# One ordered weight queue and half-by-half opening passes in a recurrent-attention kernel that is bound by the PE

## The chip, the cores and the metric

The kernel runs on one core of one Trainium2 chip. The metric is device time in microseconds (us), the median over several executions. Executions of one and the same kernel differ by up to 8 us of 1260 here (0.6%), so differences of a few us are read in two ways: from ratios over interleaved rounds with a 95% interval, and from fixed landmarks in the trace of one execution. PE is the matmul engine, DVE the vector engine, ACT the scalar engine, SP the engine that issues most DMAs. The granted clock is the share of its full speed at which the PE was allowed to run.

## The reference

A layer norm, a recurrent attention with 8 memory tokens over 64 segments of 32 tokens, a residual, then a gated feed-forward with its own norm and residual. What matters is the recurrence: the memory of a segment is the attention output of the one before.

```python
for s in range(n_seg):                       # 64 segments, strictly in order
    xs = x[:, s * seg_len:(s + 1) * seg_len, :]
    h = concatenate([mem, xs], axis=1)       # 8 memory tokens + 32 tokens, 640 wide
    q, k, v = h @ Wq, h @ Wk, h @ Wv         # 32 heads of 128, bfloat16
    p = softmax(where(mask, q @ k.T * scale, -1e9))
    o = (p @ v) @ Wo
    mem = o[:, :M, :]                        # feeds the next segment
    outs.append(o[:, M:, :])
```

Wq, Wk, Wv and Wo are 5.24 MB each, 21 MB together. No segment can be finished before all four are on the chip.

## The kernel before

A small scheduler records every operation with the tiles that it reads and writes, and turns that into semaphore waits; so an operation waits for exactly the data it names. Each weight is loaded in two halves (heads 0 to 15 and 16 to 31). The opening loads:

```python
    for g in range(4):                                   # memory tokens, first on the sync queue
        dma(wtok[1][32 * g:32 * g + M, :, :], mem0_ap..., r=[("wtok", 1)], w=[("wtok0", g)])
    x0 = oTe[:]...
    ln1_load(-1, xt, ("xt",))                            # token rows 0..63
    ln1_load(0, x0, ("oTe", 0))                          # token rows 64..191
    srcs = (A_Wq, A_Wk, A_Wv)
    qs = ("sp", "act")
    for j in (1, 0, 2):                                  # K, Q, V
        for i in range(2):                               # halves: one on each queue
            dma(W[:, j, :, 2048 * i:2048 * i + 2048], srcs[j]..., w=[("W", j, i)], eng=qs[i])
    for i in range(2):
        dma(Wo[:, 16 * i:16 * i + 16, :], A_Wo..., w=[("Wo", i)], eng=qs[i])
```

The opening passes project three groups of tokens (the rows of segments 0 and 1, and pass 0: the 8 memory tokens with 24 rows of later segments, the riders, that fill up its 32 rows) with K, Q and V. One pass uses both halves of a weight at once, with one weight load for both; so nothing starts before both halves have landed:

```python
    for j in (1, 0):                                     # K, then Q
        for n, (a, ks) in enumerate(ex_act + [(a0, k0)]):
            project(a, ks, j, (0, 1), bks)               # both halves
            to_tok(bks[0], t, "act"); to_tok(bks[1], t + 1, "dve")
            trans8(tok[t], ..., bk)                      # waits for the two copies
            ...                                          # evacuate to K or Q storage
    for n, (a, ks) in enumerate(ex_act + [(a0, k0)]):
        project(a, ks, 2, (0, 1), bks)                   # V
        to_v(...); to_v(...)
    ...
    for s in range(NSEG):
        ...                                              # (s > 0: the projections of this segment)
        scores(s); exp_mem(); exp_x()
        pv_mem(s); trans_om(s)                           # memory values, normalized, transposed
        wo_pass(oT[par], ..., T1)                        # output projection: needs Wo half 0, then half 1
        to_act(s + 1, B(T1), ...)                        # DVE transpose: the memory of segment s + 1
```

The DVE transpose in `to_act` (into the tile TBf) is the landmark of this text: it ends the opening when it starts for segment 1, and there is one for each later segment.

The softmax here doesn't subtract the row's maximum and nothing guards it: scores larger than these inputs give would overflow.

## Time and profile before

| | before |
|---|---|
| median of 3 executions | 1268.34 us (1266.53 to 1270.35) |
| profiled span | 1262.6 us |
| first projection matmul | 30.88 us |
| first output projection | 64.50 to 68.46 us |
| transpose for segment 1, for segment 2 | 68.52, 83.32 us |
| transpose for segment 63 (954.1 us after that for segment 2) | 1037.44 us |

The page of the kernel before: busy time of each engine, then the busy tenths of the PE and of the DMA engines in 40 slices of 31.6 us each, then the chain that ended last.

```profile
PE 1176.5 (93%) x31431; PEld 661.4 (52%) x29111; DVE 611.0 (48%) x1497; ACT 408.4 (32%) x775; POOL 26.6 (2%) x94
...
PE   0889999999999999999999999999999997999998
...
DMA  9801000010110101010111010100000025110100
...
PE 86%; DMA 4%; DVE 4%; ACT 3%; issue 1%; SPq 1%; POOL 0%; DVEq 0%; ACTq 0%; POOLq 0%
```

The PE is the limit nearly everywhere. The exception is the first slice, where it does nothing and the DMA is at 9 tenths. The timeline of the opening (start in us, duration, engine or issuing queue, line, operation, tile; in brackets the idle time before it and what ended it):

```profile
0.83 0.42 ACTq L304 DMA_DIRECT2D W<-in_A_Wk_dram  x1
...
5.15 3.04 SPq L304 DMA_DIRECT2D wtok<-in_A_mem_dram  x4
...
9.45 0.43 SPq L304 DMA_DIRECT2D W<-in_A_Wk_dram  x1
...
30.88 0.62 PE L345 MATMUL ps<-W,act_r 128*32 128x512 bf16 x4 [8.53 <-DMA W<-in_A_Wk_dram]
...
64.50 3.96 PE L546 MATMUL ps<-Wo,oT 128*32 128x160 bf16 x128 [0.38 <-DVE oT L380]
...
68.52 0.35 DVE L466 STREAM_TRANSPOSE TBf<-ps 128x160 f32<-128x160 f32 x1 [4.08 <-PE ps L546]
```

The activation queue issues its half of K at 0.83 us and the sync queue its half only at 9.45 us, because its memory-token loads wait for a memset and are issued first. By then the other queue holds halves of Q, V and Wo too, and the second half of K shares the engines with them until 30.88 us.

The windows view of the same kernel (stretch, its length, busy us of PE, PEld, DVE, ACT, POOL with counts, granted clock, DMA share, GB/s):

```profile
6.00:8.00 2.00, 0.00 (x0) 0.00 (x0) 0.00 (x0) 0.00 (x0) 0.00 (x0) 1.00 1.01 401
16.00:28.00 12.00, 1.16 (x10) 0.74 (x10) 4.96 (x18) 0.99 (x4) 0.00 (x0) 1.00 1.03 410
48.00:56.00 8.00, 6.42 (x115) 2.17 (x64) 1.67 (x3) 3.03 (x4) 0.00 (x0) 1.00 1.07 363
57.00:58.50 1.50, 1.50 (x36) 0.39 (x16) 0.69 (x1) 0.30 (x1) 0.00 (x0) 1.00 0.15 55
58.50:60.00 1.50, 1.50 (x36) 0.36 (x16) 0.51 (x1) 0.60 (x1) 0.00 (x0) 1.00 0.00 0
64.50:67.50 3.00, 3.00 (x92) 3.00 (x96) 0.00 (x0) 0.00 (x0) 0.00 (x0) 0.50 0.41 106
```

The DMA is saturated, on one queue (6 to 8 us) as on two. Two lines will matter later: at 57 us the rate collapses but a tail at a share of 0.15 goes on to 58.5; and the first output projection ran at a granted clock of 0.50, after a stretch in which the PE had several short waits (the longest 1.11 us).

### The profile page before, as it was taken

What the parts mean: (1) busy time and instruction counts of PE and PEld (TensorE: products, weight loads), DVE (VectorE), ACT (ScalarE), POOL (GpSimd) and SP (SyncE); (2) the same over time, 40 slices, a digit from 0 to 9 for tenths busy, and PEclk for the clock granted to TensorE, in tenths of its full rate; (3) what the DMA queues carried; (4) which work ended last, traced back from release to release, by engine and by line L of the source; (5) the groups of instructions that cost most, each with busy time, mean ns of one, the idle gap of its engine ahead of it and who ended that gap; (6) DMA issues with size and microseconds to landing.
All of it is one profiled execution on the core that took longest, in us unless ns stands there. A gap on an engine that the chain in (4) does not pass through costs nothing.

```text
span 1262.6 us, 64636 instructions
## 1 busy us (share of the span) xinstructions
PE 1176.5 (93%) x31431; PEld 661.4 (52%) x29111; DVE 611.0 (48%) x1497; ACT 408.4 (32%) x775; POOL 26.6 (2%) x94
## 2 busy tenths in 40 slices
PE   0889999999999999999999999999999997999998
PEld 0255555555556555555555555555555554455454
DVE  2244545454545454555555555454545442543522
ACT  0323333333333333333333333333333321321311
POOL 1000000000000000000000000000000000000000
PEclk9999999999999999999999999999999998999999
DMA  9801000010110101010111010100000025110100
GB/s 364 310 21 24 21 23 21 23 23 22 23 24 21 25 19 25 21 44 19 43 22 44 21 44 20 24 20 23 20 21 20 19 99 183 37 63 22 43 21 21
DMA packets 47819, 60.03 MB, mean 48 GB/s; under 512 B 20224, under 2 KB 36288, under 8 KB 47552
## 3 DMA queue, kind: packets, MB, share of 16 engines
q1 hardware_dynamic: 43520, 45.41, 12.6%
q10 hardware_dynamic: 4032, 10.49, 2.2%
q8 instruction: 237, 3.88, 1.3%
q14 instruction: 30, 0.25, 0.1%
HBM read 36.79 MB, written 6.55 MB: 34 GB/s over the span
## 4 chain that ended last, share of the span: by engine, by line
PE 86%; DMA 4%; DVE 4%; ACT 3%; issue 1%; SPq 1%; POOL 0%; DVEq 0%; ACTq 0%; POOLq 0%
PE ps L345 32%; PE ps L546 12%; PE ps L331 9%; PE ps L884 9%; PE ps L364 6%; PE ps L912 5%; PE ps L488 3%; PE ps L372 2%; PE ps L558 2%; PE ps L521 2%; DVE TBf L466 2%; DMA W<-in_A_Wk_dram 2%; PE ps L583 2%; ACT Kr L378 1%; ACT Qr L378 1%
## 5 line engine op out<-in xcount | busy, mean ns | idle before, releaser
L345 PE MATMUL ps<-W,act_r 128*32 128x512 bf16 x6460 | 447.2, 381 | 39.0 <-DVE act_r L467 12.6
L345 PEld LDWEIGHTS ps<-W,act_r 128*32 128x32 bf16 x6460 | 162.9, 96 | 286.0 <-issue 84.4
L380 DVE CAST tok<-ps 128x512 bf16<-128x512 f32 x161 | 110.9, 689 | 154.8 <-PE ps L345 78.3
L378 ACT ACTIVATE tok<-ps 128x512 bf16<-128x512 f32 x161 | 95.9, 596 | 229.7 <-PE ps L331 187.8
L546 PE MATMUL ps<-Wo,oT 128*32 128x160 bf16 x8448 | 163.8, 236 | 3.1 <-issue 2.6
L546 PEld LDWEIGHTS ps<-Wo,oT 128*32 128x32 bf16 x8448 | 148.6, 98 | 12.7 <-issue 4.5
L331 PE MATMUL ps<-W,act_r 128*32 128x512 bf16 x1420 | 138.8, 381 | 0.0
L364 PEld LDWEIGHTS ps<-ident,tok 128*128 128x128 bf16 x1288 | 72.2, 98 | 48.5 <-issue 24.2
L364 PE MATMUL ps<-ident,tok 128*128 128x128 bf16 x1288 | 89.1, 220 | 4.7 <-DVE tok L380 4.7
L604 ACT ACTIVATE oT<-ps 128x768 bf16<-128x768 bf16 x64 | 51.9, 811 | 124.4 <-PE ps L372 124.4
L345 PE MATMUL ps<-W,act_e 128*32 128x512 bf16 x900 | 89.6, 381 | 0.1
L331 PE MATMUL ps<-W,act_e 128*32 128x512 bf16 x900 | 89.2, 379 | 0.0
L378 ACT ACTIVATE Qr<-ps 128x512 bf16<-128x512 bf16 (+3 forms) x110 | 69.1, 658 | 57.4 <-DVE Qr L380 45.4
L596 DVE TENSOR_TENSOR ox<-ps,rx 128x512 bf16<-128x512 f32 x128 | 82.4, 685 | 2.2
L899 DVE TENSOR_TENSOR hT<-g,ps 128x512 bf16<-128x512 bf16 (+1 forms) x56 | 37.8, 686 | 74.7 <-PE ps L884 53.1
L466 DVE STREAM_TRANSPOSE TBf<-ps 128x160 f32<-128x160 f32 x64 | 22.4, 350 | 100.7 <-PE ps L546 100.6
L884 PE MATMUL ps<-xn2T,Wu 128*128 128x512 bf16 x260 | 66.7, 388 | 4.2 <-DMA Wu<-in_B_W_up_dram 4.2
L884 PE MATMUL ps<-xn2T,Wg 128*128 128x512 bf16 x260 | 66.6, 388 | 3.1 <-ACT g L897 3.1
L912 PE MATMUL ps<-Wd,hT 128*128 128x320 bf16 x448 | 68.1, 300 | 0.0
L378 ACT ACTIVATE wtok<-ps 128x160 bf16<-128x160 f32 x64 | 19.5, 304 | 138.7 <-DVE TBf L466 122.4
L897 ACT ACTIVATE g<-ps 128x512 bf16<-128x512 f32 (+1 forms) x56 | 32.3, 594 | 97.1 <-PE ps L884 97.1
L380 DVE CAST Vp<-ps 128x512 bf16<-128x512 f32 x64 | 44.3, 692 | 27.8 <-PE ps L345 26.4
(88 smaller groups left out, 1169.5 us busy)
## 6 DMA issues: line engine op xcount, KB each, us to landing
Vr<-Vp SPq DMA_DIRECT2D x124, 48.8 KB
xt<-in_A_x_dram SPq DMA_DIRECT2D x30, 160.0 KB
Vr<-Vp SPq DMA_DIRECT2D x128, 32.5 KB
attn_d<-wtok SPq DMA_DIRECT2D x256, 7.5 KB
W<-in_A_Wk_dram ACTq DMA_DIRECT2D x1, 2560.0 KB
W<-in_A_Wq_dram ACTq DMA_DIRECT2D x1, 2560.0 KB
W<-in_A_Wv_dram ACTq DMA_DIRECT2D x1, 2560.0 KB
Wo<-in_A_Wo_dram ACTq DMA_DIRECT2D x1, 2560.0 KB
```

Of the source, the lines that this page charges most:

```text
L331: return pe.add_instruction(mybir.InstMatmult(name=nc.get_next_instruction_name(), engine=mybir.EngineType.PE, ins=[pe.lower_ap(rhs), pe.l ...
L345: ins = pe.matmul(*a, start=(c == 0), stop=(c == DC - 1), skip_group_check=True)
L364: ins = pe.matmul(bank_bf(b)[:, k * 128:(k + 1) * 128], t[:, (k % 4) * 128:(k % 4 + 1) * 128], ident[:, :], is_transpose=True)
L378: add("act", lambda a: a.activation(dst, src, ACTF.Copy), r=r, w=w)
L380: add("dve", lambda v: v.tensor_copy(dst, src), r=r, w=w)
L466: add("dve", lambda v: v.transpose(TBf[:].rearrange("p c t -> p (c t)"), src), r=[wkey], w=[("TBf",)])
L488: i = pe.matmul(o, lh, Qr[:, h, q, :], start=True, stop=True, skip_group_check=True)
L546: i = pe.matmul(bank(bk)[32 * gg:32 * gg + 32, 0:160], src[:, hb, :], w[:, gg], start=(hb == 0), stop=(hb == 31), skip_group_check=True)
L596: add("dve", lambda v, kh=kh: v.tensor_tensor(ox[:, :, kh, :], src[:, :, kh, 0:128], ap(rx, kh, [[2, 4], [0, 128]]), ALU.mult), r=[B(b0 + ...
L604: add("act", lambda a: a.activation(oT[par][:, :, M:32].rearrange("p (k g) q -> p g k q", g=4), src[:, :, :, 0:RID], ACTF.Copy), r=[B(bk)] ...
L884: ins = pe.matmul(bank(bk), w[:, c, lo:lo + 128], xn2T[par][:, c, :], start=(c == 0), stop=(c == DC - 1))
L912: i = pe.matmul(bank(bk)[:, 0:320], hT[par][p0:128, j, u * 128:(u + 1) * 128], Wd[p0:128, j, hf * 320:(hf + 1) * 320], start=(j == 0), sto ...
```

## The change

Its intent: bring the data in the order in which it is used. Token rows go first, then all weights in one queue (sync) in the order K, Q, V, output weights; the memory tokens go to the activation queue, and their tiles are cleared on the DVE so that they wait for nothing slow. The opening passes then use each half as it lands, on three groups of accumulators, and the scores and exponentials of segment 0 stand ahead of the values, so that they no longer lie between the last value pass and the output projection.

```diff
+    for i in range(2):
+        add("dve", lambda v, i=i: v.memset(wtok[i][:], 0.0), w=[("wtok", i)])
...
-        add("pool", lambda p, i=i: p.memset(wtok[i][:], 0.0), w=[("wtok", i)])
...                                   (memory-token loads: moved behind the rows, eng="act")
-    qs = ("sp", "act")
     for j in (1, 0, 2):
         for i in range(2):
             dma(W[:, j, :, 2048 * i:2048 * i + 2048],
                 srcs[j]...,
-                w=[("W", j, i)], eng=qs[i])
+                w=[("W", j, i)])
     for i in range(2):
-        dma(Wo[:, 16 * i:16 * i + 16, :], A_Wo..., w=[("Wo", i)], eng=qs[i])
+        dma(Wo[:, 16 * i:16 * i + 16, :], A_Wo..., w=[("Wo", i)])
...
     for j in (1, 0):
-        for n, (a, ks) in enumerate(ex_act + [(a0, k0)]):
-            ...
-            project(a, ks, j, (0, 1), bks)
-            to_tok(bks[0], t, "act")
-            to_tok(bks[1], t + 1, "dve")
-            ...
-            trans8(tok[t], ("tok", t), tok[t + 1], ("tok", t + 1), bk)
-            ...
+        for n, (a, ks) in enumerate(groups):
+            project(a, ks, j, (0,), gbanks[n][:1])
+            if n < 2:
+                to_tok(gbanks[n][0], 2 * n, "act")
+        for n, (a, ks) in enumerate(groups):
+            project(a, ks, j, (1,), gbanks[n][1:])
+            if n < 2:
+                to_tok(gbanks[n][1], 2 * n + 1, "dve")
+        for n in range(2):
+            opening_back(j, n, (P2, P3)[n])
+        to_tok(P0, 0, "act")
+        to_tok(P1, 1, "dve")
+        opening_back(j, 2, P2)
+    scores(0)
+    exp_mem()
+    exp_x()
+    vbanks = (BQ, (T0, T1), (P2, P3))
+    for i in range(2):
+        for n, (a, ks) in enumerate(groups):
+            ...
+            project(a, ks, 2, (i,), vbanks[n][i:i + 1])
+            to_v(vbanks[n][i], t, i, key, ("act", "dve")[(i + n) % 2])
...                                   (in the loop: scores only if s > 0)
```

A half pass has its own weight load for each matmul, where a whole pass shared one between the halves: 3 weights x 3 groups x 20 = 180 weight loads more, all before segment 1. By count two semaphore waits fall away, so the PE has 178 instructions more.

## The prediction

> **What bounds the kernel now.** 1268.34 us (profiled span 1262.6). The page has PE busy 93%, and the chain of waits is 86% PE: a serial recurrence at the PE's pace. The change touches only the opening. In the timeline the PE's first projection waits for the K weights until 30.88 us; opening passes fill 30.88 to 60.8; the first output projection runs 64.50 to 68.50, and the transpose that starts segment 1 is at 68.52. Everything later is unchanged, so the question is where that 68.52 goes.
>
> Why 30.88: each weight's halves sit on two queues. The activation queue issues its half of K at 0.83; the sync queue waits for pool memsets (5.15), issues four memory-token loads (3.04 us) and the rows, and K's other half at 9.45, which then shares the engines with Q and V halves. The windows show DMA saturated (share about 1.0, 362 to 410 GB/s) from 4 to 57 us: 21 MB of weights. The order is wrong, not the bandwidth. The Trainium skill ("DMA: Bandwidth & Descriptors", Issuing engines are not separate DMA queues) says DMAs of all issuers share the same 16 engines, so one queue should carry as much as two; this trace agrees, with 391 to 401 GB/s from 4 to 10 us, mainly one queue active.
>
> **After, estimated from those rates.** Rows issued near 0.8 us land by 4 (before: 16.1). A Q, K or V half is 2.62 MB, 6.6 us at 397 GB/s: K lands at 10.5 and 17, Q at 23.5 and 30, V at 37 and 43. Output weights come last; alone they ran at 363 GB/s (48 to 56), 7.2 us a half: 50.5 and about 57.5 to 58.
>
> A half-pass of one group is 20 matmuls, 1.08 us (2.1 at half clock); three groups take 3.3 us against 6.6 per landing, so the PE idles and is often at the low clock. The transposes and evacuations of K and Q (3.5 us) fit in the gaps. The last V pass ends at 46 to 48; memory values, normalization and transposes (before: 62.59 to 64.50) end near 49.5. So the first output-projection half waits for its weights until 50.5, the second until 58. **The gain is capped by the end of the weight stream, not by PE order**: of 20 us gained at the first matmul, about 11 come back as waits for weights.
>
> The last half is 64 matmuls, 1.2 us warm, 2.0 at half clock (before, the pass took 4.00 us at a granted clock of 0.50). So the transpose starts at about 60: 8.5 us earlier. After some 6 us of waiting, segment 1 loses 0.5 to 1 us at the low clock. Net gain about 8 us, 0.6%.
>
> Extra weight loads (halves no longer share one) overlap matmuls; rider copies wait behind the output weights but are read two segments later.
>
> **Prediction** 1260.3 us, range 1257.0 to 1264.5. Faster by over 2%: 0.02; within 2%: 0.97; slower: 0.01.
>
> **Right if the profile shows:** first projection at 10 to 12 us; PE waits for W between halves every 6.6 us; a wait of 4 to 7 us for output weights inside the first output projection; DMA share near 1.0 until 57 to 58; the first transpose of new memory at 59 to 61; later segments unchanged (about 15 us).
>
> **Wrong if:** one queue carries clearly less than two (at 350 GB/s the stream ends near 63 and the gain shrinks); waits hold the PE at half clock until V passes end after 57; rows or memory tokens arrive late; or later clock changes (1030 to 1090 us, windows at 0.71 to 0.95) fall differently, 1 to 2 us either way.

## The result, and the profile after

Ratios here are the mean time of one kernel's fast runs over that of the other's of the same rounds, so not quite the ratio of the quoted medians.

| | before | after |
|---|---|---|
| median of 4 | 1267.65 us (1266.53 to 1270.35) | 1262.43 us (1259.34 to 1264.47) |
| ratio, 95% interval | | 0.9952 (0.9931 to 0.9973) |
| profiled span | 1262.6 us | 1262.7 us (its execution was the slowest of the four) |
| first projection matmul | 30.88 us | 11.94 us |
| transpose for segment 1 | 68.52 us | 62.09 us |
| transpose for segment 2 | 83.32 us | 78.60 us |
| from there to the transpose for segment 63 | 954.1 us | 958.5 us |

The gain is about 6 us of 1268 (mean 1268.05 against 1262.17), half a per cent: real, and within 2%. The page after:

```profile
PE 1179.2 (93%) x31413; PEld 666.8 (53%) x29291; DVE 611.7 (48%) x1499; ACT 408.1 (32%) x775; POOL 26.1 (2%) x92
...
PE   5599999999999999999999999999999987999998
...
DMA  9900000100000000010101010001000026110100
...
PE 83%; DMA 5%; DVE 4%; ACT 3%; SPq 3%; issue 2%; DVEq 0%; ACTq 0%
```

The PE works in half of the first slice now, and is idle for half of the second, where it was busy for 8 tenths. The timeline of the opening:

```profile
0.81 0.59 SPq L305 DMA_DIRECT2D xt<-in_A_x_dram  x1
...
2.07 1.18 SPq L305 DMA_DIRECT2D W<-in_A_Wk_dram  x2
...
11.94 4.92 PE L346 MATMUL ps<-W,act_r 128*32 128x512 bf16 x60 [1.92 <-DVE act_r L468]
...
18.04 3.42 PE L346 MATMUL ps<-W,act_r 128*32 128x512 bf16 x60 [1.17 <-DMA W<-in_A_Wk_dram]
...
44.90 5.11 PE L346 MATMUL ps<-W,act_r 128*32 128x512 bf16 x60 [2.67 <-DMA W<-in_A_Wv_dram]
...
52.13 1.29 PE L547 MATMUL ps<-Wo,oT 128*32 128x160 bf16 x64 [0.51 <-DMA Wo<-in_A_Wo_dram]
...
59.72 2.32 PE L547 MATMUL ps<-Wo,oT 128*32 128x160 bf16 x64 [6.30 <-DMA Wo<-in_A_Wo_dram]
...
62.09 0.35 DVE L467 STREAM_TRANSPOSE TBf<-ps 128x160 f32<-128x160 f32 x1 [10.14 <-PE ps L547]
...
62.72 4.05 PE L346 MATMUL ps<-W,act_r 128*32 128x512 bf16 x40 [0.68 <-DVE act_r L468]
```

Here is where the 19 us went that the first matmul came earlier. The passes wait for four of the six halves of K, Q and V, 1.1 to 2.7 us each (by the profile the first half of K came no later than the memory tokens, and the first half of V before the PE was free), and then the second half of the output projection waits 6.30 us for the last weights, which land at 59.7 us. Nothing that the PE does before that moment can bring the landing forward. After the wait 64 matmuls take 2.32 us, where the 64 before it took 1.29 at 52.13, and the first 40 of segment 1 take 4.05 us where the same group takes 2.34 elsewhere. The windows view says why:

```profile
48.00:56.00 8.00, 3.81 (x110) 2.20 (x102) 1.48 (x4) 0.60 (x1) 0.00 (x0) 0.93 1.07 362
56.00:58.00 2.00, 0.00 (x0) 0.00 (x0) 0.00 (x0) 0.00 (x0) 0.00 (x0) 0.50 1.08 313
58.00:59.50 1.50, 0.00 (x0) 0.00 (x0) 0.00 (x0) 0.00 (x0) 0.00 (x0) 0.50 0.52 137
59.50:62.00 2.50, 2.28 (x64) 2.00 (x64) 0.00 (x0) 0.00 (x0) 0.00 (x0) 0.50 0.09 30
62.00:66.00 4.00, 3.32 (x36) 1.24 (x36) 0.53 (x2) 0.60 (x1) 0.00 (x0) 0.50 0.00 0
```

The DMA stays saturated to about 58 us and then has a tail, as before; the granted clock falls to 0.50 in the wait and stays there to 66 us.

### The profile page after: what moved, and what is told of

Read it like the earlier page. It is cut to its first block, busy times and chain, and to the rows that moved or that the text cites. A ratio compares the mean times of both kernels' runs of the same rounds, so it can differ in the third digit from the quotient of the medians.

```text
span 1262.7 us, 64802 instructions
## 1 busy us (share of the span) xinstructions
PE 1179.2 (93%) x31413; PEld 666.8 (53%) x29291; DVE 611.7 (48%) x1499; ACT 408.1 (32%) x775; POOL 26.1 (2%) x92
## 4 chain that ended last, share of the span: by engine, by line
PE 83%; DMA 5%; DVE 4%; ACT 3%; SPq 3%; issue 2%; DVEq 0%; ACTq 0%
PE ps L346 31%; PE ps L547 12%; PE ps L332 8%; PE ps L898 8%; PE ps L365 6%; PE ps L926 5%; SPq L305 3%; PE ps L489 3%; DMA Wo<-in_A_Wo_dram 2%; PE ps L559 2%; PE ps L373 2%; PE ps L522 2%; PE ps L584 2%; DVE TBf L467 2%; ACT Kr L379 1%
## 5 line engine op out<-in xcount | busy, mean ns | idle before, releaser
L346 PE MATMUL ps<-W,act_r 128*32 128x512 bf16 x6640 | 458.1, 386 | 38.8 <-DVE act_r L468 14.3
L346 PEld LDWEIGHTS ps<-W,act_r 128*32 128x32 bf16 x6640 | 170.8, 97 | 287.2 <-issue 82.9
L332 PE MATMUL ps<-W,act_r 128*32 128x512 bf16 x1240 | 120.6, 379 | 0.0
L379 ACT ACTIVATE Qr<-ps 128x768 bf16<-128x768 bf16 (+3 forms) x110 | 69.1, 658 | 62.5 <-DVE Qr L381 50.4
L898 PE MATMUL ps<-xn2T,Wg 128*128 128x512 bf16 x250 | 63.5, 384 | 4.8 <-issue 2.6
```

The source lines that it names most:

```text
L332: return pe.add_instruction(mybir.InstMatmult(name=nc.get_next_instruction_name(), engine=mybir.EngineType.PE, ins=[pe.lower_ap(rhs), pe.l ...
L346: ins = pe.matmul(*a, start=(c == 0), stop=(c == DC - 1), skip_group_check=True)
L379: add("act", lambda a: a.activation(dst, src, ACTF.Copy), r=r, w=w)
L898: ins = pe.matmul(bank(bk), w[:, c, lo:lo + 128], xn2T[par][:, c, :], start=(c == 0), stop=(c == DC - 1))
```

## The experiments

Theory A: the gain comes from the order of the loads and is capped by the end of the weight stream; the order of the passes has slack. Theory B: the half-by-half order is what makes early weights usable. Theory C came up when the traces were compared: the stretch from segment 2 to the end, whose code nobody changed, was 4.4 us longer in the profile after, with PE waits that the profile marks as issue. All results are in this table; the sections follow. The landmarks are of the one profiled execution of each kernel. Runs e1 to e4 shared one chip, e5 to e12 another (e5 to e8 and e9 to e12 were timed apart, each beside before), so ratios to before are compared, not times. Timed over 5 rounds each.

| run | ratio to before (95%) | first projection | transpose, segment 1 | segment 2 | segment 2 to 63 |
|---|---|---|---|---|---|
| before | 1 | 30.88 | 68.52 | 83.32 | 954.1 |
| after | 0.9952 (0.9931 to 0.9973) | 11.94 | 62.09 | 78.60 | 958.5 |
| e1, loads of after, passes of before | 0.9964 (0.9944 to 0.9984) | 18.22 | 61.77 | 76.57 | 952.8 |
| e2, passes of after, loads of before | 0.9987 (0.9970 to 1.0003) | 31.25 | 65.48 | 80.28 | 956.7 |
| e3, after with half of Wo's bytes | 0.9895 (0.9876 to 0.9914) | 11.82 | 53.71 | 68.51 | 956.4 |
| e4, after with dummy matmuls in the wait | 0.9960 (0.9941 to 0.9979) | 12.18 | 61.19 | 75.98 | 956.5 |
| e5, before with rows first, two queues | 0.9972 (0.9953 to 0.9991) | 25.36 | 65.73 | 80.52 | 958.9 |
| e6, after with 78 PE instructions more | 0.9968 (0.9949 to 0.9986) | 12.20 | 62.38 | 78.39 | 955.6 |
| e7, before with 178 PE instructions more | 1.0019 (1.0000 to 1.0037) | 30.99 | 69.30 | 84.09 | 958.2 |
| e8, e4 with 26 PE instructions more | 0.9953 (0.9932 to 0.9973) | 11.90 | 62.49 | 77.28 | 954.6 |
| e9, after with the scores behind the values | 0.9947 (0.9931 to 0.9963) | 12.06 | 62.48 | 78.37 | 954.3 |
| e10, after again | 0.9953 (0.9934 to 0.9972) | 11.90 | 62.05 | 78.35 | 957.4 |
| e11, e1 again | 0.9961 (0.9942 to 0.9980) | 18.13 | 62.31 | 78.05 | 953.3 |
| e12, e4 again | 0.9936 (0.9919 to 0.9953) | 11.89 | 61.85 | 76.65 | 955.9 |

All results were correct, with e3's reported as correct too although half of the output weights were replaced by others, so its result cannot be the reference's. Perhaps the attention output is small beside the residual at the tolerance used.

### e1: the loads alone

The kernel before with the load section and the DVE memsets of after; the passes untouched.

```diff
-    for g in range(4):
-        dma(wtok[1]..., mem0_ap...)                      # first, sync queue
     ln1_load(-1, xt, ("xt",))
     ln1_load(0, x0, ("oTe", 0))
+    for g in range(4):
+        dma(wtok[1]..., mem0_ap..., eng="act")
-    ... weight halves with eng=qs[i]
+    ... weight halves, all on the sync queue
```

> The loads of after (rows first, memory tokens on the activation queue, all weights in one ordered sync queue, token tiles cleared on VectorE) with the opening passes of before (whole weights, values before scores). Theory A (the gain comes from the order of the loads and is capped by the end of the weight stream at about 59.7 us): the passes run K 18 to 29, Q 32 to 43, V 45 to 53 us, the first output projection starts near 56.5, waits 2 us or less for the last output weights instead of 6.3, so the PE keeps its clock; segment 1's transpose at 61 to 62 us, segment 2's at 76 to 77 (after: 62.09 and 78.60; before: 68.52 and 83.32). Time 6 to 8 us under before, at least as fast as after. Theory B (the half-by-half order is what makes the early weights usable): the passes end after 60 us, segment 2's transpose at 80 us or later, time at most 3 us under before.

The timeline of e1:

```profile
18.22 0.62 PE L346 MATMUL ps<-W,act_r 128*32 128x512 bf16 x4 [8.19 <-DMA W<-in_A_Wk_dram]
...
57.99 3.73 PE L547 MATMUL ps<-Wo,oT 128*32 128x160 bf16 x128 [0.38 <-DVE oT L381]
```

The first projection starts 6.3 us later than in after (it needs both halves of K) and the opening ends no later: 61.77 us for segment 1, 76.57 for segment 2. The output projection begins at 57.99 and is done 3.73 us later, without waiting for weights. The ratio, 0.9964, is level with that of after. Theory A holds: the loads alone give the whole gain that can be measured, and the slower passes just use up the wait. ("The loads" is four edits at once: rows first, memory tokens on the other queue, DVE memsets, one queue for the weights; e5 takes a part of them.) The pass ended the wait later than expected (57.99, not 56.5), and it ran at a low clock all the same.

### e2: the passes alone

The kernel after with the load section and the memsets of before: the edit is the reverse of e1's.

> The opening passes of after with the loads of before (two queues, rows behind the memory tokens). First projection stays at 30.9 us in both theories. Theory A: the denser order and the hidden scores save a few us, because the PE does not go cold before the output projection: passes end near 59.8, output projection at about 62 at full clock, segment 1's transpose 64 to 65, segment 2's 79 to 80 us (before 83.32): time 3 to 5 us under before, so the two parts each give most of the gain and do not add up. Theory B (order needs the early loads, alone it gives nothing): segment 2's transpose at 82 to 84, time within 1.5 us of before.

The opening gains 3.0 us by the landmark (80.28 against 83.32), less than the 3.3 to 4.3 expected; one 1.07 us wait marked issue fell into the output projection. The time gains 0.13%, which the interval does not tell from nothing. Of the 3.0 us, 2.8 are the earlier start of the output projection (61.74 against 64.50); the pass itself took 3.7 us with that wait, at the full clock, against 3.96 at the low one. So the expectation that each part gives most of the gain was half wrong: the loads do, the passes only by the landmark and not in the time. The parts do not add up: 6.75 us (e1) and 3.0 us (e2) by the landmark, and 4.7 together.

### e3: half the bytes of the output weights

After, loading 8 of 16 heads of each half of Wo and using them twice; the same matmuls.

```diff
-        dma(Wo[:, 16 * i:16 * i + 16, :], A_Wo...[:, 16 * i:16 * i + 16, :], w=[("Wo", i)])
+        dma(Wo[:, 16 * i:16 * i + 8, :], A_Wo...[:, 16 * i:16 * i + 8, :], w=[("Wo", i)])
...
-                    w = Wo[:, head(hb // 4, hb % 4), :]...
+                    w = Wo[:, head(hb // 4, hb % 4) // 16 * 16 + head(hb // 4, hb % 4) % 8, :]...
```

> After, but only half of each half of the output weights is loaded and used twice: 2.6 MB less in the stream, result wrong on purpose, same number of matmuls. Theory A (the end of the weight stream caps the gain): stream ends near 52.5 us, the wait inside the first output projection goes from 6.3 us to under 1, no cold clock after it; segment 1's transpose at 54 to 55.5, segment 2's at 69 to 70.5 us; time 8 to 10 us under after. Rival (the PE's chain of opening passes is the limit): segment 2's transpose stays at 76 or later, time within 3 us of after.

The timeline of e3:

```profile
50.47 1.29 PE L547 MATMUL ps<-Wo,oT 128*32 128x160 bf16 x64 [0.38 <-DVE oT L381]
...
52.37 1.29 PE L547 MATMUL ps<-Wo,oT 128*32 128x160 bf16 x64 [0.61 <-DMA Wo<-in_A_Wo_dram]
...
54.34 2.34 PE L346 MATMUL ps<-W,act_r 128*32 128x512 bf16 x40 [0.67 <-DVE act_r L468]
```

The wait inside the output projection falls from 6.30 to 0.61 us, both half passes take 1.29 us, segment 1 starts at the full clock, and segment 2's transpose comes 10.1 us earlier than in after. Not all of the 10.1 us is owed to the bytes: from 17 us on the PE never fell to the low clock in e3's opening, and V's last half pass took 3.42 us where it took 5.11 in after, which is at most 1.7 us. The time is 1.05% under before, more than twice the gain of after; against after by the ratios it is about 7 us, a little short of the 8 to 10 expected. This is the direct evidence that the end of the weight stream caps the change: with fewer bytes and the same number of PE instructions the rest of the gain appears.

### e4 and e12: a PE kept busy in the wait

After, with 26 matmuls of the identity against the K weights into a free bank, between the halves of segment 0's output projection. The result is not touched.

```diff
-        wo_pass(oT[par], ..., T1)
+        if s == 0:
+            wo_pass(oT[par], ..., T1, (0,))
+            add("pe", spin, r=[("ident",), ("W", 1, 0)], w=[B(P2)])   # 26 matmuls, 128x512
+            wo_pass(oT[par], ..., T1, (1,))
+        else:
+            wo_pass(oT[par], ..., T1)
```

> After, with 26 dummy matmuls (128x512) into a free bank between the two halves of the first output projection, filling 5.6 of the 6.3 us wait. Theory: the low granted clock after the wait (0.50 from 56 to 66 us) is due to the idle PE and costs 1.1 us in the second half pass and 1.7 us in segment 1. Then the second half pass takes 1.25 us instead of 2.32 and segment 1 takes 14.8 instead of 16.5: segment 1's transpose at 61.0, segment 2's at 75.8 us, time 2.5 to 3 us under after, result right. Rival (the low clock comes with the DMA load or the time since start): the clock stays at 0.50 there and the time is that of after.

The windows of e4 in the stretches where after has a clock of 0.50:

```profile
56.00:62.00 6.00, 4.58 (x83) 2.40 (x85) 0.53 (x2) 0.00 (x0) 0.00 (x0) 1.00 0.56 154
62.00:66.00 4.00, 4.00 (x128) 1.85 (x112) 1.76 (x4) 0.60 (x1) 0.00 (x0) 1.00 0.01 4
```

The DMA load is the same and the clock is 1.00: the low clock comes from the idle PE. The second half pass takes 1.29 us and segment 1 takes 14.8 us instead of 16.5; segment 2's transpose is 2.6 us earlier than in after, as expected. The Trainium skill, "TensorE: Matmul & The Clock Gate", Part 1, says that the PE's clock falls to half after an idle window of about 3.4 us; the trace agrees on the half clock but not on the length: in after the clock fell at 55.99 us, 2.6 us after the last matmul had ended (53.42), and in before it fell at 64.39 us although no wait of the PE in the 3.4 us before was longer than 1.11 us (the PE was busy for 1.3 us of them). Several short waits were enough. The ratio to before (0.9960) does not show the 2.5 to 3 us under after that I had expected, but after itself had not run on that chip; so the run was repeated beside it.

> After with the dummy matmuls in the wait, again, beside after on one chip: segment 2's transpose at 76 to 77.5 us (the earlier value depends on whether the PE is warm when the dummy matmuls begin), time 1 to 2.5 us under after, level with the queue order alone within 1 us.

In e12 the PE was already at the low clock when the dummy matmuls began (the first half pass took 2.33 us), they took longer, and the opening gained 1.7 us instead of 2.6 against e10. The mean time was 1256.96 us against 1258.90 for after on the same chip, 1.9 us less, and the ratio to before, 0.9936, is the lowest of the versions with a right result; its interval overlaps that of after, so the 1.9 us are not shown. The same kernel as e4 had 0.9960.

### e5: rows first, but two queues

Before, with the token rows issued ahead of the memory tokens on the sync queue and the DVE memsets; weights stay split over two queues.

```diff
-    for g in range(4):
-        dma(wtok[1]..., mem0_ap...)
     ln1_load(-1, xt, ("xt",))
     ln1_load(0, x0, ("oTe", 0))
+    for g in range(4):
+        dma(wtok[1]..., mem0_ap...)
```

> Before with one thing changed: the sync queue issues the token rows first, then the memory tokens, then its halves; both queues and the whole-weight passes stay. It asks whether one ordered queue matters or only that the sync queue no longer starts its weights at 9.45 us. Theory A (what counts is that both halves of K are ahead of the rest): both halves land together at about 17 to 18 us instead of 30.9, the first projection starts there, the stream still ends at 57 to 60 us, segment 1's transpose at 61 to 63, segment 2's at 76 to 78 us, time within 2 us of the kernel that has the queue order alone (segment 2's transpose at 76.57). Rival (one ordered queue is what gains): first projection after 22 us, segment 2's transpose at 80 or later.

This went against my expectation. The timeline of e5:

```profile
2.48 12.09 ACTq L305 DMA_DIRECT2D Wo<-in_A_Wo_dram  x1
...
5.08 0.45 SPq L305 DMA_DIRECT2D W<-in_A_Wk_dram  x1
...
15.33 0.44 DVE L317 TENSOR_SCALAR xt<-xt,mv,rs 64x640 bf16<-64x640 bf16 x1 [8.00 <-ACT rs L314]
...
25.36 0.62 PE L346 MATMUL ps<-W,act_r 128*32 128x512 bf16 x4 [5.53 <-DMA W<-in_A_Wk_dram]
```

The first projection starts at 25.4, not at 18, though the sync queue issues its half of K at 5.08 instead of 9.45: that half, 2.62 MB, took until 25.36 us, about 130 GB/s of the 404 that all transfers had then, so it shared the engines with the halves of the other queue, and K's second half was not ahead of Q's first. A second thing shows: ACT is held by its fourth load's issue for 12.09 us, and the normalization of rows that had landed by 6.2 us waits 8.00 us for ACT. Here that cost nothing beyond what K's late half cost, but it could in a kernel whose rows are the limit. So rows first is not enough: segment 2's transpose is at 80.52 us, 2.5 us behind the loads alone on the same chip (e11) and 4.0 behind e1; the times do not tell them apart (0.9972 against 0.9961). That it is the one queue is likely but not isolated: in e5 the memory tokens also stay on the sync queue, whose weights start 4.2 us after those of the other queue (5.08 against 0.84). Two queues that start together were not run. The Trainium skill, "DMA: Bandwidth & Descriptors", Issuing engines are not separate DMA queues, says that DMAs of all issuers run on the same 16 engines and interleave. The traces agree on the bandwidth (before: 401 GB/s with one queue, 410 with two; after, on one queue: 410 from 12 to 40 us). What the queues decide is which bytes come first.

### e9: the scores behind the values again

After, with the three calls for segment 0 back in the segment loop.

```diff
-    scores(0)
-    exp_mem()
-    exp_x()
...
-        if s > 0:
-            scores(s)
+        scores(s)
...
```

> After with one part undone: segment 0's scores and exponentials stand behind the value passes again, as in before. Theory A (the opening waits for the last output weights whatever the PE order): the first output-projection half starts near 54 us instead of 52.1, the wait for the last weights shrinks from 6.3 to about 4.5 us, segment 1's transpose stays at 61.5 to 62.5 us, time within 1.5 us of after on the same chip. Rival (hiding the scores gains its 1.9 us): segment 1's transpose at 63.5 to 64.5 us.

The first half pass starts at 53.25 us instead of 52.13, the wait for the last weights is 5.56 us instead of 6.30 (5.04 in e10), and the second half starts at 60.10. Segment 1's transpose is at 62.48, segment 2's at 78.37. Ratio 0.9947 against 0.9953 for after on the same chip. This part of the change is worth nothing here: it lies ahead of a wait that absorbs it.

### e10 and e11: after and the loads alone, side by side

Both kernels unchanged, on one chip.

> After, unchanged, beside the others on one chip. Segment 1's transpose at 61.5 to 62.5 and segment 2's at 78 to 79 us; time 4 to 6 us under before. If the places of the PE's issue stalls belong to the program and only their lengths to the run, they are again near 157, 189, 330, 645 and 960 us, with other lengths; if they are chance they are elsewhere.

> The queue order alone again (same kernel as before under another label), beside after on one chip: segment 2's transpose 2 us earlier than after (76.6 against 78.6), time 5 to 7 us under before and 0 to 2.5 us under after. If the half-by-half order gains anything on top of the queue, after is faster instead.

After repeated its ratio (0.9953). The loads alone gave 0.9961, a mean 1.0 us over after on this chip where I had expected 0 to 2.5 us under; the earlier run had them 2 us ahead by the landmark, this one 0.3 us. In e11 the PE's value passes were warm and ended earlier, so the kernel did wait for the last weights (2.22 us, to 59.93) and ran segment 1 partly at the low clock. What can be said is that the two do not differ by more than these runs resolve, about 0.2%.

### e6, e7 and e8: where the later PE waits sit

Between segment 2 and the end no line of code changed, and yet the first profile after lost 4.4 us there. In the windows from 70 to 1030 us the waits of the PE that the profile marks as issue, meaning that it waited for nothing it shows (total us, times, longest), are in before:

```profile
PE ps L546 <- issue: 1.7, 4, 0.6
PE ps L558 <- issue: 1.3, 1, 1.3
...
PE ps L345 <- issue: 0.6, 2, 0.4
```

and in after:

```profile
PE ps L559 <- issue: 3.7, 3, 1.5
PE ps L547 <- issue: 2.7, 6, 0.8
PE ps L346 <- issue: 1.6, 3, 0.8
```

The sums are 3.6 and 8.0 us, which is the 4.4 us that were lost. The trace also records the DMAs that fetch PE instructions: 237 of 16,384 bytes in before, 238 in after. Each of the 19 such waits in these windows of the two traces ended 1.2 to 1.6 us after the end of one of these fetches. Most of the waits (5 of 7 and 9 of 12) stand in the output projections, the densest code (the 128 matmuls of a pass with their 128 weight loads take 2.4 us), while no two fetches started less than about 3.3 us apart.

Theory C: where a fetch block begins is set by the number of instructions ahead of it, and the opening of after has 178 PE instructions more. A block holds about 256 (the median between two fetches was 259). So 78 more instructions should bring back the places of before, and 178 more in before should give the places of after. The padding is tiny matmuls on the identity, issued while the PE waits for its first rows.

```diff
+    def pad(pe):
+        for _ in range(39):                  # e6; 89 in e7 (on before), 13 in e8 (on e4)
+            ins = pe.matmul(bank(BQ[0])[0:32, 0:32], ident[:, 0:32], ident[:, 0:32], start=True, stop=True)
+        return ins
+    add("pe", pad, r=[("ident",)], w=[B(BQ[0])])
     row_stats(xt, ("xt",), 64)
```

> After, with 78 more PE instructions (39 tiny matmuls on the identity, each with its weight load) issued while the PE waits for its first rows. The change had added 178 PE instructions to the opening (180 weight loads, two waits fewer); with 78 more the later code is displaced by 256 instructions, the size of one 16 KB instruction fetch, against before. Theory C (the later stalls marked issue[...] sit where a fetch block begins in the dense output projection, so the displacement sets them): stalls fall on the places of before, their sum goes from 12.2 us to about 4.5, segment 2's transpose stays at 78 to 79 us, and from there to the last segment's transpose 953 to 955 us (before 954.1, after 958.5). Time 3 to 5 us under after. Rival (the stalls are chance of a run): the sum stays where it falls, the stretch stays 956 to 959.

> Before, with 178 more PE instructions (89 tiny matmuls with weight loads) while the PE waits for its first rows, as many as the change adds. The opening keeps its times (first projection 30.9, segment 2's transpose 83.3 us). Theory C: the stalls move to the places of after (one in segment groups at 314 us distance in the four-quarter output projection), their sum goes from 4.5 to 8 to 12 us, the stretch from segment 2's to the last transpose from 954 to 956 to 958.5 us, time 2 to 5 us over before. Rival (chance): stretch as before, time within 1 us.

> After with the dummy matmuls of the kernel that keeps the PE busy in the wait for the last output weights (52 PE instructions) and 26 more at the start, so that the displacement against before is again 256. If both theories hold: segment 2's transpose at 76.0 us, stretch to the last transpose 953 to 955, time 3 us under the kernel with the dummy matmuls only and 6 us under after, about level with the queue order alone. If theory C fails: as the kernel with the dummy matmuls only (stretch 956.5).

One wait in the four-quarter output projection of each kernel shows the result. The count at the end of the operation is the number of matmuls of that pass that were still to come after the wait. Before, and after with 78 more:

```profile
209.44 0.45 PE L558 MATMUL ps<-Wo,oTe 128*32 128x320 bf16 x7 [1.27 <-issue]
```

```profile
203.71 0.45 PE L559 MATMUL ps<-Wo,oTe 128*32 128x320 bf16 x7 [0.96 <-issue]
```

After, after again (e10), and before with 178 more (e7):

```profile
330.40 0.72 PE L559 MATMUL ps<-Wo,oTe 128*32 128x320 bf16 x14 [0.90 <-issue]
```

```profile
329.36 0.72 PE L559 MATMUL ps<-Wo,oTe 128*32 128x320 bf16 x14 [0.76 <-issue]
```

```profile
334.43 0.72 PE L558 MATMUL ps<-Wo,oTe 128*32 128x320 bf16 x14 [0.77 <-issue]
```

The padding moved the wait to the same instruction, 7 or 14 matmuls from the end, two segment groups apart. The other places follow too: e10 has them near 156, 188, 329, 642 and 956 us where after has 157, 189, 330, 645 and 961. So the places belong to the program, and what sets them is the number of instructions ahead.

The lengths are another matter. Over 70 to 1030 us the sum is 5.0 us in e6 and 6.3 in e7, between before and after; one wait that all six kernels with the places of before share, 6 matmuls ahead of the end of an output projection near 580 us, is 0.38 us long in before, 0.37, 0.36, 0.36 and 0.49 in e1, e6, e8 and e11, and 1.20 in e5. The stretch from segment 2 to 63 has a mean of 954.9 us over the six profiles with the places of before (before, e1, e5, e6, e8, e11: 952.8 to 958.9) and 956.9 over the six with the places of after (after, e2, e3, e7, e9, e10: 954.3 to 958.5). The timed runs do not settle it: e7 is 0.19% over before, at the edge of its interval, as theory C wants; e6 should then be faster than after and is not (0.9968 against 0.9953 on the same chip), and e8 (0.9953) is not faster than e12 (0.9936). What does go along with the stretch is the sum itself: over the 14 profiles it is lowest in before, e1, e8 and e11 (3.6 to 4.3 us, with stretches of 952.8 to 954.6) and highest in after and e5 (8.0 and 7.3 us, with 958.5 and 958.9), and the correlation of the two is 0.91. So the total length of these waits goes with most of the difference between one profile's stretch and another's, and the lengths differ between executions even at the same places. The displacement is shown; that it costs time, perhaps 2 us, is not.

## Why the prediction was right

- **The size, 1260.3 us, and the range 1257.0 to 1264.5.** Measured 1262.43. I had forecast about 8 us of gain; it was 5.9 by the means of the first runs and again 5.8 by those of e10 (1264.66 to 1258.90). By the landmark of segment 2 it was only 4.7. The two sizes that were off (below) both took from the forecast gain; the range was wide enough for both.
- **First projection at 10 to 12 us, PE waits between halves every 6.6 us.** Right: 11.94 us, though the first halves of K and V brought no wait. From K's second half (18.04) to V's second half (44.90) are 4 halves in 26.9 us, 6.7 us each, against 6.6 forecast.
- **The gain is capped by the end of the weight stream, not by the PE order.** Right, and the central point. e3 takes the bytes away and frees the rest of the gain; e1 and e9 undo parts of the PE order and lose nothing.
- **A wait of 4 to 7 us inside the first output projection.** Right: 6.30 us, and 5.0 to 5.6 us in e9 and e10.
- **The first transpose at 59 to 61 us.** Missed by 1.1 us: 62.09. The term that was mis-sized is the landing of the last weights, "57.5 to 58", which was 59.7. The rate of the stream was forecast well: by the packet records of after, half of all bytes of K, Q and V (three halves) had landed by 23.74 us, against 23.5 forecast, and the rate falls at 57.5 us. What was left out is the tail: the PE waits for the last packet (that of V ended at 44.36 us, and the PE went on at 44.90). It was released 1.0 us (K's second half, 18.04), 2.0 (Q's first, 25.54) and 1.9 us (V's second, 44.90) later than forecast, and 1.7 us or more for the last weights. In before I took 57 us as the end of the stream, where the rate falls, but the windows above show a share of 0.15 on to 58.5 us.
- **Segment 1 loses 0.5 to 1 us at the low clock.** The mechanism is right (e4 takes the loss away), the size was off: 1.7 us (16.51 between the transposes for segments 1 and 2 against 14.80 before), because the clock came back only after 66 us.
- **"Everything later is unchanged."** True of the code and, within what these runs resolve, of the time; not true of the positions of the instruction fetches, which I had not thought of. In the first pair of profiles the difference was 4.4 us, nearly as much as the gain of the opening, and it hid it: the two profiled spans are equal. That pair by itself would have led to a false conclusion. The timed runs did not show such a loss.
- **Extra weight loads overlap.** Right as far as it goes: the half passes take 3.42 us for 60 matmuls at the full clock, 57 ns each, no more than 40 matmuls in 2.34 us elsewhere.

No version was clearly better than after. The loads alone (e1, e11) are level with it at a smaller edit. Dummy matmuls in the wait (e12) gave the best mean, 1.9 us under after. None of these has its first transpose before 61 us, and the last weights land near 59.7 where the PE waited for them.

## What to carry to other kernels

When a chain of work needs all of a data set before its first full result, earlier arrival of its first parts gains only until the end of the stream becomes the wait; find that end in the trace before (the landing of its last packet, not the moment when the rate falls: 2 us apart in after) and compute the gain from there. Order the loads in one queue by first use: here two queues had no more bandwidth (410 GB/s, as with one) and shared it between data needed now and data needed later. And when two profiles disagree far from the edit, compare landmark by landmark and profile the same kernels again before explaining it.

## What the Trainium skill lacked or had wrong

- "Runtime: NRT & Kernel Launch", Instruction fetch mechanics, says that the engine's instruction memory is refilled in 16 KiB blocks of 256 instructions, and that crossing a block boundary is "mostly hidden". The trace agrees on the block (237 fetches of 16,384 bytes) but not always on the hiding: the PE lost 3.6 to 8.0 us between 70 and 1030 us, in waits of up to 1.5 us; the 19 in before and after ended 1.2 to 1.6 us after a fetch, where a pass of 256 PE instructions takes 2.4 us. The page does not say that the number of instructions ahead decides where such waits fall (e6, e7).
- "DMA: Bandwidth & Descriptors", Issuing engines are not separate DMA queues, calls the issue time "usually small relative to the DMA itself". An ACT that issues its fourth 2.6 MB load was held for 7.05 us in before and 12.09 us in e5, where its next activation stood behind it. The page's section lacks this.
- The same page, Specifications, gives 512 bytes as the smallest transfer for line rate. Weights in rows of 4,096 bytes streamed at 410 GB/s here and the output weights, in rows of 1,280 bytes, at 361 to 365, with the share of the engines near 1.0 in both. No run tests whether the row length is the reason.
- "TensorE: Matmul & The Clock Gate", Part 1, gives about 3.4 us of idle before the clock halves. Here it halved 2.6 us after the last matmul (after) and with no wait over 1.11 us (before), as told under e4.
